# A second series of warm-up products, and the third FFN step in an output bank, in a chunked-attention plus FFN kernel on one core

## Chip, cores and metric

The kernel runs on one core of a Trainium2 chip. The metric is device time in microseconds (us). Before the change the median of three runs is 878.25 us.

## What is computed

Attention inside chunks of 64 positions, then a two-layer FFN on its output (8 batches, 8 heads, 576 positions, head size 64; 4608 tokens, model width 512, FFN width 2048):

```python
scores = (1 / sqrt(64)) * q_c @ k_c.T              # per batch, head and chunk of 64
attn = exp(scores - max); attn = attn / (sum + 1e-9)
x = (attn @ v_c), tokens x 512                     # 4608 x 512
h = x @ w_in                                       # 512 x 2048
g = h if h >= 1; 0 if h <= -1; (h + 1)**2 / 4 between
out = g @ w_out                                    # 2048 x 512
```

## The kernel before

**Tiles.** Tokens go in 9 tiles of 512 (`NTILE`). Each tile has an attention part of 4 head groups (two heads each, `g`) and an FFN part of 16 steps (`j`). An FFN step makes a 128-wide slice of h with 12 TensorE products (`ffn_in`, L532; four groups `kc`, one for each head group, of three products each, since fp32 numbers are split into a high and a low part: xh, xl, and two halves of the weight), the function on it (ScalarE L539 and L542, VectorE L543, then the split into gh, gl at L552 and L553), and two steps later 12 products into four output banks (`ffn_out`, L567, banks ps_o0 to ps_o3).

**Attention of a head group.** Of the first tile: q and k are transposed on TensorE (`flip`, L361, four transposes) and copied to SBUF by ScalarE (L376); 16 small score products (L392, which the trace counts as 32) go into one half of a pair of banks, VectorE takes the maximum (L446) and subtracts it (L462), ScalarE makes the exponential (L465), VectorE the sum and its reciprocal (L471 to L473), GpSimd multiplies (L478). The result e is transposed back (`attn_turn_back`, L361) and copied (L501), 16 value products (L413) go into the other half of the same pair of banks, and ScalarE and VectorE split what comes out into xh (L516) and xl (L517). Two pairs of banks alternate in the first tile: ps_a for even groups, ps_o2 and ps_o3 for odd ones. Of the second tile the exponentials come as eight pieces with their sums (L455). From the third tile on, transposes are done by VectorE.

**Weights.** Each of the 32 weight blocks (wi0 to wi15, wo0 to wo15) arrives as pairs of 32-bit words and is prepared once, on ScalarE (L259, L265, L284) and VectorE (L262, L269, L274, L288; L288 writes the low part and is the last). Until then several tiles of the first attention tile (names `first_...`) lie where late weights will be.

**Order.** `Plan` holds every piece of work with an estimated cost and its needs; its `emit` walks an estimated clock and puts the pieces into the queue of each engine, the earliest first. So each engine's order is fixed at build time, and each engine takes its queue in order. Where TensorE would have nothing to do by the estimate, before the first FFN product, `emit` puts in warm-up products on the identity matrix (L681, into ps_h0, result unused). The order in which the pieces are handed to `Plan` breaks ties: a piece handed in earlier goes first.

In words, before: head group g's value products are handed in right after the scores of group g + 1; the transposes back of the first tile use ps_h1, the bank of the second FFN step; FFN step n uses ps_h0 or ps_h1 by parity; weights are prepared in the order wi0, wi1, wo0, wi2, wo1, wi3, ...

Of the kernel before, what the change touches and what calls it, by code (L numbers as in the profile page):

```python
# [17 lines left out]
class Plan:  # L18
# [9 lines left out]
    def __init__(self):  # L28
        self.parts = []
        self.writer = {}  # L30
        self.readers = {}

    def add(
        self, engine, cost, emit, reads=(), writes=(), lag=0.0, columns=0, port=False, moving=0.0
    ):
        n = len(self.parts)
        needs = {self.writer[k] for k in (*reads, *writes) if k in self.writer}
        for k in writes:
            needs.update(self.readers.pop(k, ()))
            self.writer[k] = n  # L40
        for k in reads:
            self.readers.setdefault(k, []).append(n)
        needs.discard(n)
        self.parts.append((engine, cost, emit, needs, lag, columns, port, moving, writes))

# [15 lines left out]
    def emit(self, filler):  # L61
# [20 lines left out]

        fill_engine, fill_cost, fill_emit, fill_key, fill_columns = filler
        filling = True
        self.columns = {}
        for _ in range(len(parts)):
            while True:
# [12 lines left out]
                start, e = best  # L100
                if filling and free[fill_engine] < start:
                    fill_emit()
                    free[fill_engine] = self.products_end(free[fill_engine], fill_cost, fill_columns)
                    continue
# [3 lines left out]
            n = heapq.heappop(now[e])  # L108
            _, cost, emit, _, lag, columns, port, moving, writes = parts[n]
            filling = filling and fill_key not in writes  # L110
            emit()
            if port:
                start = max(start, port_free)
# [16 lines left out]
def kernel(  # L130
# [15 lines left out]
    nc = tc.nc  # L146
# [18 lines left out]

    FLIPPED = 2

    BATCH = (0, 1, 2, 3, None, 4, 5, 6, 7)
# [131 lines left out]

    def load_rows(dst, src, t, g):

        dst = dst.rearrange("p (c d) -> p c d", d=D)
        for j in range(2):
            nc.sync.dma_start(
                out=dst[j * C:(j + 1) * C],
                in_=heads_rows(src, t, 2 * g + j).rearrange("c p d -> p c d"),
            )

    def load_blocks(dst, src, t, g):  # L310


        dst = dst.rearrange("p (c e d) -> p c e d", e=2, d=Q)
        for j in range(2):
            for i in range(2):
                r = (2 * j + i) * Q
                rows = heads_rows(src, t, 2 * g + j)[:, :, i * Q:(i + 1) * Q]
                if BATCH[t] is not None:
                    nc.sync.dma_start(  # L319
                        out=dst[r:r + Q],  # L320
# [3 lines left out]
                for e in range(2):  # L324
                    nc.sync.dma_start(
                        out=dst[r:r + Q, :, e, :],
                        in_=rows[:, e * Q:(e + 1) * Q, :].rearrange("c p d -> p c d"),
                    )

    def load_values(dst, src, t, g):  # L330

        for h in range(2):
            rows = heads_rows(src, t, 2 * g + h)
            into = dst[:, h * HALF:(h + 1) * HALF].rearrange("p (n d) -> p n d", d=D)
            if BATCH[t] is not None:
                nc.sync.dma_start(out=into, in_=rows.rearrange("(n r) p d -> (r p) n d", r=2))
                continue
            for r in range(2):
                nc.sync.dma_start(
                    out=into[r * C:(r + 1) * C],  # L340
# [3 lines left out]
    def load_heads(t, g, which="qkv"):  # L344
        for n, src, bufs in (("q", q, q_bufs), ("k", k, k_bufs), ("v", v, v_bufs)):
# [5 lines left out]
            if BATCH[t] is None:  # L351
                parts *= 2
            plan.add(
                "sp", 0.67 * parts, lambda load=load, dst=dst, src=src: load(dst, src, t, g),
                (), (key,), lag=2.1, moving=2.2 if load == load_blocks else 1.35,
            )

    def flip(ps, src):
        for u in range(NS):
            cols = slice(u * P, (u + 1) * P)  # L360
            nc.tensor.transpose(out=ps[:, cols], in_=src[:, cols], identity=ident)  # L361

    def attn_turn(t, g):
        for n, (name, bufs, src_bufs, dst_bufs) in enumerate(
# [4 lines left out]
            if t >= FLIPPED:  # L369
# [5 lines left out]
            plan.add("pe", 0.45, lambda src=src, ps=ps: flip(ps, src), (skey,), (pkey,), columns=T)  # L375
            plan.add("act", 0.48, lambda ps=ps, dst=dst: nc.scalar.copy(out=dst, in_=ps),  # L376
                     (pkey,), (dkey,))

# [56 lines left out]
    def attn_softmax(t, g):  # L435
# [39 lines left out]
        plan.add("dve", 0.35 if sums else 1.05, norm, (ekey,), (skey,))  # L475
        on_pool = t < 2
        eng = nc.gpsimd if on_pool else nc.vector
# [4 lines left out]
    def attn_turn_back(t, g):  # L482
# [14 lines left out]

        if t < FLIPPED:
            pkey, ps = h_banks[1] if t == 0 else a_banks[0]
            plan.add("pe", 0.45, lambda: flip(ps, e), (ekey,), (pkey,), columns=T)  # L500
# [21 lines left out]
    def ffn_in(t, j):  # L522
        n = t * NF + j
        pkey, ps = h_banks[n % 2]
        rkey, r = r_bufs[n % 2]
# [82 lines left out]
    for j in range(NF):  # L608
        order.append(("wo", j))
        if j + 2 < NF:  # L610
            order.append(("wi", j + 2))
    for g in range(NP + 1):
        if g < NP:
            attn_turn(0, g)
            attn_products(scores_of(0, g))
            attn_softmax(0, g)
        if g > 0:
            attn_turn_back(0, g - 1)
            attn_products(values_of(0, g - 1))
            attn_split(0, g - 1)  # L620
    loads = [o for o in order if o not in first_loads]
# [12 lines left out]
    prepare("wi", 0)  # L634
    prepare("wi", 1)

    LAG = 2
    todo = list(order)
    for t in range(NTILE + 1):
# [39 lines left out]

    def warm():  # L680
        nc.tensor.matmul(out=h_banks[0][1][:, :P], lhsT=ident, rhs=ident, start=True, stop=True)  # L681

    plan.emit(("pe", 0.215, warm, "ps_h0", 512))


# [29 lines left out]
```

## Time and profile before

| | us |
|---|---|
| timed runs, median (lowest to highest) | 878.25 (877.94 to 878.71) |
| the profiled execution's own time | 878.0 |
| its span in the trace | 876.2 |
| TensorE busy | 860.7 (98%) |
| VectorE busy | 445.0 (51%) |
| ScalarE busy | 382.4 (44%) |

The span is the time from the first to the last instruction of the trace; the device time of the same execution is 1.8 us longer. The span starts with loads, the attention of the first tile and the preparation of the weights; then FFN products follow each other to the end, with the attention of the next tile between them.

### The profile page before, as it was taken

What the parts mean: (1) busy time and instruction counts of PE and PEld (TensorE: products, weight loads), DVE (VectorE), ACT (ScalarE), POOL (GpSimd) and SP (SyncE); (2) the same over time, 40 slices, a digit from 0 to 9 for tenths busy, and PEclk for the clock granted to TensorE, in tenths of its full rate; (3) what the DMA queues carried; (4) which work ended last, traced back from release to release, by engine and by line L of the source; (5) the groups of instructions that cost most, each with busy time, mean ns of one, the idle gap of its engine ahead of it and who ended that gap; (6) DMA issues with size and microseconds to landing.
All of it is one profiled execution on the core that took longest, in us unless ns stands there. A gap on an engine that the chain in (4) does not pass through costs nothing.

```text
span 876.2 us, 14898 instructions
## 1 busy us (share of the span) xinstructions
PE 860.7 (98%) x5942; PEld 707.5 (81%) x5942; DVE 445.0 (51%) x758; ACT 382.4 (44%) x703; POOL 9.9 (1%) x14
## 2 busy tenths in 40 slices
PE   9689999999999999999999999999999999999998
PEld 8577888888888888888888888888888888888886
DVE  4999995444444445444544454444444444423222
ACT  4899964333333333333433333334333433333332
POOL 1001000000000000000000000000000000000000
PEclk9899999999999999999999999999999999999999
DMA  8998215222322224222422243223222311001001
GB/s 195 344 307 238 48 27 116 48 42 42 88 50 39 49 49 97 49 50 49 97 49 48 47 88 53 46 43 89 49 43 46 75 35 25 13 1 49 0 1 49
DMA packets 250821, 62.86 MB, mean 72 GB/s; under 512 B 235904, under 2 KB 244096, under 8 KB 250752
## 3 DMA queue, kind: packets, MB, share of 16 engines
q1 hardware_dynamic: 250752, 61.91, 31.4%
q8 instruction: 47, 0.77, 0.4%
q14 instruction: 22, 0.18, 0.1%
HBM read 45.09 MB, written 9.44 MB: 62 GB/s over the span
## 4 chain that ended last, share of the span: by engine, by line
PE 90%; DVE 3%; DMA 1%; ACT 1%; SPq 1%; issue 1%; POOL 0%; POOLq 0%; DVEq 0%; ACTq 0%
PE ps_o L567 43%; PE ps_h L532 43%; PE ps_a L413 2%; PE ps_a L392 1%; DMA words_wo<-in_moe_w_out_dram 1%; DVE tmp L269 1%; SPq L244 1%; PE ps_a L361 1%; DVE tmp L274 0%; DMA k_sb<-in_k_dram 0%; SPq L319 0%; POOL e L478 0%; ACT tmp L259 0%; DVE mx L446 0%; DVE tmp L262 0%
## 5 line engine op out<-in xcount | busy, mean ns | idle before, releaser
L532 PE MATMUL ps_h<-xh,parts_wi 128*128 128x512 f32 x1152 | 384.9, 394 | 2.1 <-ACT xh L516 1.7
L567 PE MATMUL ps_o<-parts_wo,gh 128*128 128x512 f32 x1152 | 356.1, 390 | 0.0
L532 PEld LDWEIGHTS ps_h<-xh,parts_wi 128*128 128x128 f32 x1152 | 216.8, 188 | 48.8 <-ACT xh L516 1.9
L567 PEld LDWEIGHTS ps_o<-parts_wo,gh 128*128 128x128 f32 x1152 | 216.3, 188 | 44.8
L543 DVE SCALAR_TENSOR_TENSOR r<-ps_h,r 128x512 f32<-128x512 f32 x144 | 98.0, 681 | 266.7 <-ACT r L542 266.7
L532 PE MATMUL ps_h<-xl,parts_wi 128*128 128x512 f32 x576 | 225.1, 391 | 0.8 <-DVE xl L517 0.8
L567 PE MATMUL ps_o<-parts_wo,gl 128*128 128x512 f32 x576 | 224.3, 389 | 0.0
L539 ACT ACTIVATE r<-ps_h 128x512 f32<-128x512 f32 x144 | 86.3, 599 | 285.5 <-PE ps_h L532 285.5
L552 ACT CAST gh<-r 128x512 fp32r<-128x512 f32 x144 | 89.8, 623 | 153.7 <-PE ps_o L567 116.9
L553 DVE TENSOR_TENSOR gl<-r,gh 128x512 fp32r<-128x512 f32 x144 | 98.8, 686 | 109.7 <-ACT gh L552 109.4
L567 PEld LDWEIGHTS ps_o<-parts_wo,gl 128*128 128x128 f32 x576 | 108.3, 188 | 22.7
L532 PEld LDWEIGHTS ps_h<-xl,parts_wi 128*128 128x128 f32 x576 | 108.4, 188 | 22.6 <-DVE xl L517 1.1
L542 ACT ACTIVATE r<-r 128x512 f32<-128x512 f32 x144 | 91.1, 633 | 3.3
L446 DVE TENSOR_REDUCE mx<-ps_a 128x8 f32<-128x512 f32 x34 | 23.4, 690 | 24.2 <-ACT xh L516 13.3
L413 PEld LDWEIGHTS ps_a<-aT,v_sb 64*64 64x64 f32 x1056 | 18.4, 134 | 11.4 <-issue 10.9
L516 ACT CAST xh<-ps_a 128x512 fp32r<-128x512 f32 x34 | 20.0, 588 | 15.3 <-PE ps_a L392 14.6
L471 DVE TENSOR_REDUCE sm<-e 128x8 f32<-128x512 f32 x30 | 20.6, 686 | 10.9 <-ACT e L465 10.9
L413 PE MATMUL ps_a<-aT,v_sb 64*64 64x64 f32 x1056 | 22.9, 224 | 0.0
L517 DVE TENSOR_TENSOR xl<-ps_a,xh 128x512 fp32r<-128x512 f32 x34 | 22.4, 658 | 0.2 <-ACT xh L516 0.2
L392 PE MATMUL ps_a<-kT,qT 64*64 64x64 f32 x1056 | 21.4, 218 | 0.4 <-ACT kT L376 0.4
L504 DVE STREAM_TRANSPOSE x<-e 128x512 f32<-128x512 f32 x28 | 19.9, 711 | 0.9
L370 DVE STREAM_TRANSPOSE qT<-q_sb 128x512 f32<-128x512 f32 x28 | 19.7, 702 | 0.0
(81 smaller groups left out, 391.1 us busy)
## 6 DMA issues: line engine op xcount, KB each, us to landing
words_wi<-in_moe_w_in_dram SPq DMA_DIRECT2D x16, 512.0 KB, 6.8
words_wo<-in_moe_w_out_dram SPq DMA_DIRECT2D x16, 512.0 KB, 7.5
out_dram<-tmp SPq DMA_DIRECT2D x32, 256.0 KB, 2.0
v_sb<-in_v_dram SPq DMA_DIRECT2D x60, 128.0 KB, 2.8
aT<-x SPq DMA_DIRECT2D x224, 32.0 KB, 1.9
q_sb<-in_q_dram SPq DMA_DIRECT2D x96, 64.0 KB, 2.3
k_sb<-in_k_dram SPq DMA_DIRECT2D x96, 64.0 KB, 2.3
q_sb<-in_q_dram SPq DMA_DIRECT2D x12, 128.0 KB, 7.5
```

The source lines that it names most:

```text
L392: nc.tensor.matmul(out=pair[i * C:(i + 1) * C, half, n * C:(n + 1) * C], lhsT=qT[rows, at], rhs=kT[rows, at], start=True, stop=True,)
L413: nc.tensor.matmul(out=pair[h * C:(h + 1) * C, half, HALF + n * C:HALF + (n + 1) * C], lhsT=v_sb[rows, of:of + C], rhs=aT[rows, at:at + C] ...
L446: plan.add("dve", 0.6, lambda: nc.vector.tensor_reduce(out=mx4, in_=sc, axis=AX.X, op=ALU.max), pkeys, (mkey,))
L471: nc.vector.tensor_reduce(out=sm, in_=e3, axis=AX.X, op=ALU.add)
L517: plan.add("dve", 0.6, lambda: nc.vector.tensor_tensor(out=of_tokens(xl), in0=ps, in1=of_tokens(xh.bitcast(F32)), op=ALU.subtract), (*pkey ...
L532: nc.tensor.matmul(out=ps, lhsT=weight["wi", j][:, half, kc * P:(kc + 1) * P], rhs=x, start=(kc == 0 and i == 0), stop=(kc == KC - 1 and i ...
L539: plan.add("act", 0.48, lambda: nc.scalar.activation(out=r, in_=ps, func=AF.Relu, bias=0.5, scale=0.5), (pkey,), (rkey,))
L542: plan.add("act", 0.52, lambda: nc.scalar.square(out=r, in_=r), (), (rkey,))
L543: plan.add("dve", 0.6, lambda: nc.vector.scalar_tensor_tensor(out=r, in0=ps, scalar=1.0, in1=r, op0=ALU.max, op1=ALU.min), (pkey,), (rkey,))
L552: plan.add("act", 0.52, lambda: nc.scalar.copy(out=gh, in_=r), (rkey,), (ghkey,))
L553: plan.add("dve", 0.6, lambda: nc.vector.tensor_tensor(out=gl, in0=r, in1=gh.bitcast(F32), op=ALU.subtract), (rkey, ghkey), (glkey,), port ...
L567: nc.tensor.matmul(out=acc, lhsT=x[:, cols], rhs=weight["wo", j][:, half, :], start=(j == 0 and i == 0), stop=(j == NF - 1 and i == 2),)
```

## The change

1. The loads of k of the first two head groups are issued from ScalarE's queue, ahead of all its other work; SyncE's queue no longer issues them.
2. In the first tile, a head group's transpose back, value products and split are handed in two groups later instead of one (`range(NP + 2)`, `g - 2`), and the transpose back uses ps_o1 and no longer ps_h1.
3. The third FFN step (n = 2, `EARLY`) accumulates in ps_o0; later steps count two banks from there. The first product of wo0 into ps_o0 has to wait until that step has been read.
4. Weights: wi2 is prepared in front of the loop, and in the lists wi(j+2) stands ahead of wo(j).
5. The multiplication of the second tile moves from GpSimd to VectorE (`on_pool`).
6. The warm-up products may come in two series: the first as before until the first FFN product, the second into ps_o0 between the last q copy of the first tile and the opening of the third FFN step.

```diff
-        fill_engine, fill_cost, fill_emit, fill_key, fill_columns = filler
-        filling = True
+        fill_engine, fill_cost, fill_columns, fillers = filler
+        done = {None}
+
+        def fill():
+            for fill_emit, begin, end in fillers:
+                if begin in done and end not in done:
+                    return fill_emit
+            return None
...
-                if filling and free[fill_engine] < start:
-                    fill_emit()
+                if free[fill_engine] < start and fill():
+                    fill()()
...
+    EARLY = 2
...
+            issuer, queue = ("act", nc.scalar) if (n, t) == ("k", 0) and g < 2 else ("sp", nc.sync)
             plan.add(
-                "sp", 0.67 * parts, lambda load=load, dst=dst, src=src: load(dst, src, t, g),
-                (), (key,), lag=2.1, moving=2.2 if load == load_blocks else 1.35,
+                issuer, 0.67 * parts,
+                lambda load=load, dst=dst, src=src, queue=queue: load(dst, src, t, g, queue),
+                (), (key,), lag=2.1, moving=2.2 if load == load_blocks else 1.2,
             )
...
-        on_pool = t < 2
+        on_pool = t < 1
...
-            pkey, ps = h_banks[1] if t == 0 else a_banks[0]
+            pkey, ps = o_banks[1] if t == 0 else a_banks[0]
...
         n = t * NF + j
-        pkey, ps = h_banks[n % 2]
+
+        pkey, ps = o_banks[0] if n == EARLY else h_banks[(n if n < EARLY else n - EARLY - 1) % 2]
...
     for j in range(NF):
-        order.append(("wo", j))
         if j + 2 < NF:
             order.append(("wi", j + 2))
-    for g in range(NP + 1):
+        order.append(("wo", j))
+    for g in range(NP + 2):
         if g < NP:
             attn_turn(0, g)
             attn_products(scores_of(0, g))
             attn_softmax(0, g)
-        if g > 0:
-            attn_turn_back(0, g - 1)
-            attn_products(values_of(0, g - 1))
-            attn_split(0, g - 1)
+        if 1 < g:
+            attn_turn_back(0, g - 2)
+            attn_products(values_of(0, g - 2))
+            attn_split(0, g - 2)
...
     prepare("wi", 1)
+    prepare("wi", 2)
 
     LAG = 2
-    todo = list(order)
+    todo = order[1:]
...
-    plan.emit(("pe", 0.215, warm, "ps_h0", 512))
+    plan.emit(("pe", 0.215, 512, (
+        (warm(h_banks[0][1]), None, plan.written["ps_h0"][0]),
+        (warm(o_banks[0][1]), turned[0], plan.written["ps_o0"][NP]),
+    )))
```

Where it moves instructions. TensorE around the third head group's scores, before: `ps_a` holds even head groups, `first_wi12` and `first_wo13` are the transposed k and q of the later groups, `e0` the exponentials of group 0.

```order
L361 MATMUL ps_o1_114<-ident_63,first_wi14_119 128x128 x4
L681 MATMUL ps_h0_115<-ident_63 128x128 x4
L413 MATMUL ps_a_112<-aT0_78,v_sb0_72 64x64 x16
L681 MATMUL ps_h0_115<-ident_63 128x128 x2
L361 MATMUL ps_o0_113<-ident_63,first_wi15_117 128x128 x4
L681 MATMUL ps_h0_115<-ident_63 128x128 x5
L392 MATMUL ps_a_112<-first_wi12_123,first_wo13_122 64x64 x16
L361 MATMUL ps_h1_116<-ident_63,e1_77 128x128 x4
```

The same place with the change:

```order
L376 MATMUL ps_o1_114<-ident_63,first_wi14_119 128x128 x4
L704 MATMUL ps_h0_115<-ident_63 128x128 x4
L413 MATMUL ps_a_112<-first_wi12_123,first_wo13_122 64x64 x16
L376 MATMUL ps_o1_114<-ident_63,e0_76 128x128 x4
L376 MATMUL ps_o0_113<-ident_63,first_wi15_117 128x128 x4
L704 MATMUL ps_h0_115<-ident_63 128x128 x3
L376 MATMUL ps_o1_114<-ident_63,first_wi14_119 128x128 x4
L704 MATMUL ps_h0_115<-ident_63 128x128 x4
L413 MATMUL ps_o23_111<-first_wi12_123,first_wo13_122 64x64 x16
L376 MATMUL ps_o1_114<-ident_63,e1_77 128x128 x4
L434 MATMUL ps_a_112<-aT0_78,v_sb0_72 64x64 x16
```

The score products of group 2 now stand ahead of group 0's value products on ps_a, those of group 3 ahead of all value products; before, each value product came first.

TensorE from the third FFN step (parts_wi2) on, before; e0 is here the first head group of the second tile:

```order
L532 MATMUL ps_h0_115<-xh2_0_89,parts_wi2_502 128x512
L532 MATMUL ps_h0_115<-xl2_0_97,parts_wi2_502 128x512
L532 MATMUL ps_h0_115<-xh2_0_89,parts_wi2_502 128x512
L361 MATMUL ps_a_112<-ident_63,e0_76 128x128 x4
L532 MATMUL ps_h0_115<-xh3_0_91,parts_wi2_502 128x512
L532 MATMUL ps_h0_115<-xl3_0_99,parts_wi2_502 128x512
L532 MATMUL ps_h0_115<-xh3_0_91,parts_wi2_502 128x512
L567 MATMUL ps_o0_113<-parts_wo0_473,gh0_103 128x512 x2
L567 MATMUL ps_o0_113<-parts_wo0_473,gl0_105 128x512
```

The same with the change, up to that transpose of e0:

```order
L589 MATMUL ps_o1_114<-parts_wo0_534,gl0_105 128x512
L589 MATMUL ps_o23_111<-parts_wo0_534,gh0_103 128x512 x2
L589 MATMUL ps_o23_111<-parts_wo0_534,gl0_105 128x512
L589 MATMUL ps_o23_111<-parts_wo0_534,gh0_103 128x512 x2
L589 MATMUL ps_o23_111<-parts_wo0_534,gl0_105 128x512
L554 MATMUL ps_h0_115<-xh2_0_89,parts_wi3_565 128x512
L554 MATMUL ps_h0_115<-xl2_0_97,parts_wi3_565 128x512
L554 MATMUL ps_h0_115<-xh2_0_89,parts_wi3_565 128x512
L554 MATMUL ps_h0_115<-xh3_0_91,parts_wi3_565 128x512
L554 MATMUL ps_h0_115<-xl3_0_99,parts_wi3_565 128x512
L554 MATMUL ps_h0_115<-xh3_0_91,parts_wi3_565 128x512
L376 MATMUL ps_a_112<-ident_63,e0_76 128x128 x4
```

Ahead of these twelve rows stand the 12 products of wi2 (into ps_o0), the first 6 of wi3 and 2 of wo0. So all of wi3 and 9 products of wo0 now stand ahead of that transpose of e0, where before 3 products of wi2 and all of these stood behind it.

## Rows read from the trace of the kernel before

**Rows 1.** The page: busy time, share of the span, instructions of TensorE.

```profile
PE 860.7 (98%) x5942; PEld 707.5 (81%) x5942; DVE 445.0 (51%) x758; ACT 382.4 (44%) x703; POOL 9.9 (1%) x14
```

**Rows 2.** Windows: stretch, us, busy PE, PEld, DVE, ACT, POOL, granted clock, DMA share, GB/s.

```profile
25.00:30.00 5.00, 2.45 (x41) 1.54 (x39) 4.65 (x10) 4.31 (x8) 0.62 (x1) 0.94 1.20 333
30.00:35.00 5.00, 3.77 (x42) 2.93 (x43) 5.00 (x10) 4.30 (x9) 0.42 (x1) 0.50 1.06 342
35.00:40.00 5.00, 4.62 (x50) 3.64 (x49) 4.60 (x8) 4.03 (x9) 0.00 (x0) 0.87 1.06 404
...
45.00:50.00 5.00, 3.84 (x12) 3.17 (x13) 4.49 (x8) 5.00 (x11) 1.11 (x1) 0.66 0.89 290
50.00:80.00 30.00, 29.30 (x255) 23.56 (x255) 28.03 (x52) 28.78 (x77) 1.29 (x1) 1.00 1.03 318
80.00:110.00 30.00, 29.76 (x197) 23.98 (x196) 29.43 (x55) 29.09 (x69) 2.09 (x2) 1.00 0.35 63
```

**Rows 3.** Timeline, TensorE: start, us, what, count, idle time before and its releaser.

```profile
6.12 0.60 PE L361 MATMUL ps_o<-ident,q_sb 128*128 128x128 f32 x4
...
8.88 0.69 PE L392 MATMUL ps_a<-kT,qT 64*64 64x64 f32 x32
...
10.43 1.06 PE L681 MATMUL ps_h<-ident 128*128 128x128 f32 x8
...
19.05 0.69 PE L392 MATMUL ps_a<-first_wi,first_wo 64*64 64x64 f32 x32
...
24.14 0.69 PE L392 MATMUL ps_o<-first_wi,first_wo 64*64 64x64 f32 x32 [2.05 <-DVE xl L517]
...
33.15 1.13 PE L413 MATMUL ps_o<-first_wi,first_wo 64*64 64x64 f32 x32 [1.23 <-ACT first_wi L501]
...
41.36 0.50 PE L532 MATMUL ps_h<-xh,parts_wi 128*128 128x512 f32 x1 [0.36 <-DVE r L543]
...
46.16 0.84 PE L361 MATMUL ps_a<-ident,e 128*128 128x128 f32 x4 [2.47 <-POOL e L478]
...
72.15 0.66 PE L361 MATMUL ps_a<-ident,k_sb 128*128 128x128 f32 x4 [0.70 <-ACT qT L376]
...
97.46 0.40 PE L532 MATMUL ps_h<-xh,parts_wi 128*128 128x512 f32 x1
```

**Rows 4.** Timeline, VectorE.

```profile
17.88 0.68 DVE L517 TENSOR_TENSOR xl<-ps_a,xh 128x512 fp32r<-128x512 f32 x1
19.81 0.69 DVE L446 TENSOR_REDUCE mx<-ps_a 128x8 f32<-128x512 f32 x1 [1.25 <-PE ps_a L392]
...
22.07 0.69 DVE L471 TENSOR_REDUCE sm<-first_wo 128x8 f32<-128x512 f32 x1 [0.84 <-ACT first_wo L465]
...
44.36 0.20 DVE L473 RECIPROCAL sm<-sm 128x8 f32<-128x8 f32 x1
...
45.13 1.53 DVE L288 TENSOR_TENSOR parts_wo<-tmp,parts_wo 128x512 fp32r<-128x512 f32 x1
...
90.44 0.68 DVE L288 TENSOR_TENSOR parts_wi<-tmp,parts_wi 128x512 fp32r<-128x512 f32 x1
```

**Rows 5.** Timeline, ScalarE.

```profile
25.46 0.59 ACT L501 COPY first_wi<-ps_h 128x512 f32<-128x512 f32 x1 [1.91 <-PE ps_h L361]
...
41.50 0.31 ACT L455 ACTIVATE e<-ps_a,mx 128x64 f32<-128x64 f32 x1
...
43.83 0.66 ACT L552 CAST gh<-r 128x512 fp32r<-128x512 f32 x1
```

**Rows 6.** Timeline, GpSimd.

```profile
23.34 1.05 POOL L478 TENSOR_TENSOR first_wo<-first_wo,sm 128x512 f32<-128x512 f32 x1 [4.48 <-DVE sm L473]
...
44.73 1.38 POOL L478 TENSOR_TENSOR e<-e,sm 128x512 f32<-128x512 f32 x1 [14.31 <-DVE sm L473]
```

**Rows 7.** Chain that ended last: start, us, engine, tile, line, count.

```profile
85.83 2.72 PE ps_h L532 x12
```

**Rows 8.** Timeline, SyncE's queue of loads.

```profile
2.25 1.31 SPq L305 DMA_DIRECT2D k_sb<-in_k_dram  x2
```

More of the change, by code (lines that the diff above doesn't have):

```diff
@@ L31, in __init__ @@
         self.readers = {}
+        self.written = {}
     def add(
@@ L43, in add @@
         needs.discard(n)
-        self.parts.append((engine, cost, emit, needs, lag, columns, port, moving, writes))
+        for k in writes:
+            self.written.setdefault(k, []).append(n)
+        self.parts.append((engine, cost, emit, needs, lag, columns, port, moving))
+        return n
     def products_end(self, start, cost, columns):
@@ L108, in emit @@
             n = heapq.heappop(now[e])
-            _, cost, emit, _, lag, columns, port, moving, writes = parts[n]
-            filling = filling and fill_key not in writes
+            _, cost, emit, _, lag, columns, port, moving = parts[n]
             emit()
+            done.add(n)
             if port:
@@ L299, in heads_rows, with load_rows @@
         return src[:, h, T:, :]
-    def load_rows(dst, src, t, g):
+    def load_rows(dst, src, t, g, queue):
         dst = dst.rearrange("p (c d) -> p c d", d=D)
         for j in range(2):
-            nc.sync.dma_start(
+            queue.dma_start(
                 out=dst[j * C:(j + 1) * C],
@@ L308, in load_rows, with load_blocks @@
             )
-    def load_blocks(dst, src, t, g):
+    def load_blocks(dst, src, t, g, queue):
         dst = dst.rearrange("p (c e d) -> p c e d", e=2, d=Q)
@@ L318, in load_blocks @@
                 if BATCH[t] is not None:
-                    nc.sync.dma_start(
+                    queue.dma_start(
                         out=dst[r:r + Q],
@@ L324, in load_blocks @@
                 for e in range(2):
-                    nc.sync.dma_start(
+                    queue.dma_start(
                         out=dst[r:r + Q, :, e, :],
@@ L328, in load_blocks, with load_values @@
                     )
-    def load_values(dst, src, t, g):
+    def load_values(dst, src, t, g, queue):
         for h in range(2):
@@ L335, in load_values @@
             if BATCH[t] is not None:
-                nc.sync.dma_start(out=into, in_=rows.rearrange("(n r) p d -> (r p) n d", r=2))
+                queue.dma_start(out=into, in_=rows.rearrange("(n r) p d -> (r p) n d", r=2))
                 continue
             for r in range(2):
-                nc.sync.dma_start(
+                queue.dma_start(
                     out=into[r * C:(r + 1) * C],
@@ L375, in attn_turn @@
             plan.add("pe", 0.45, lambda src=src, ps=ps: flip(ps, src), (skey,), (pkey,), columns=T)
-            plan.add("act", 0.48, lambda ps=ps, dst=dst: nc.scalar.copy(out=dst, in_=ps),
-                     (pkey,), (dkey,))
+            copy = plan.add(
+                "act", 0.48, lambda ps=ps, dst=dst: nc.scalar.copy(out=dst, in_=ps),
+                (pkey,), (dkey,),
+            )
+            if t == 0:
+                turned[n] = copy
     def scores_of(t, g):
@@ L678, with warm @@
                 ffn_split(t, j)
-    def warm():
-        nc.tensor.matmul(out=h_banks[0][1][:, :P], lhsT=ident, rhs=ident, start=True, stop=True)
-    plan.emit(("pe", 0.215, warm, "ps_h0", 512))
+    def warm(bank):
+        return lambda: nc.tensor.matmul(
+            out=bank[:, :P], lhsT=ident, rhs=ident, start=True, stop=True
+        )
+    plan.emit(("pe", 0.215, 512, (
+        (warm(h_banks[0][1]), None, plan.written["ps_h0"][0]),
+        (warm(o_banks[0][1]), turned[0], plan.written["ps_o0"][NP]),
+    )))
 _INS = ['q', 'k', 'v', 'moe_w_in', 'moe_w_out']
```

1 line of the change is left out of this document (added).

## Prediction

> **What bounds the kernel now.** I read the page first: TensorE is busy 860.7 of 876.2 us [rows 1]. It works nearly without a gap from the second FFN step to the end, so a change can win only what TensorE loses; the windows show where. From 50 to 110 us it stands still 0.70 and 0.24 us in 30 each [rows 2], but between 25 and 50 us it is idle for long parts, and the granted clock is below 1.00: 0.94, 0.50 and 0.87 in three neighbouring windows, and 0.66 in 45 to 50 us [rows 2]. At two levels, 2.4 and 1.2 GHz, that is 0.6 + 5.0 + 1.3 = 6.9 us at the lower one, and once more 5.0 x 0.34 / 0.5 = 3.4 us. Both follow on idle time: 2.05 us before 24.14 and more up to 33.15, and 2.47 us before 46.16 [rows 3].
>
> The timeline tells what TensorE waits for there. The third group's scores start at 19.05, the fourth's at 24.14 after 2.05 us for an xl, the last values at 33.15 after 1.23 us for a ScalarE copy, and the transpose of the second tile's first e at 46.16 after 2.47 us for GpSimd [rows 3]. These are links of one chain, attention of the first tile and then of the second tile's first group. The prepared weights don't end these waits, but VectorE is busy 4.49 to 5.00 of each 5 us shown and 28.03 and 29.43 of 30 afterwards [rows 2], so it comes next.
>
> **The change, step by step.** I walk the new order with the durations of before. Four transposes take 0.44 us to the next start and 0.60 to their end, four warm-up products 0.99 and 1.06, 16 score or value products 0.62 and 0.69 [rows 3], three FFN products 0.68 (2.72 / 4) [rows 7]; on VectorE a 128x512 operation takes 0.69 and the next starts 0.09 before its end, on ScalarE 0.59 to 0.66 and some 0.1 [rows 4, 5].
>
> *Loads.* Two k loads of 1.31 us each leave SyncE's queue [rows 8], so everything behind them is issued 2.6 us earlier. ScalarE issues them itself; the trace has no load on its queue. At SyncE's price they hold it 2.6 us from its start, before its first copy has anything to copy (the first transposes start at 6.12 [rows 3]); at twice that, 5.2 us, just not. The first warm-up products are as many as before, so transposes still start at 6.12; then only one warm-up product stands between k and q instead of four, and the first scores move from 8.88 to about 8.2. All of the softmax moves by this 0.7.
>
> *Values two groups later.* The third group's scores use ps_a, and before had to follow group 0's values and their xl (VectorE, 17.88 to 18.56 [rows 4]). Now they wait only for their own transposes and copies: 14.8 instead of 19.05. VectorE takes them in turn, maximum at 16.6 instead of 19.81 [rows 4]; the fourth group's scores come at 18.5 instead of 24.14, its subtraction at 20.7, exponential on ScalarE until 22.4, sum and reciprocal 1.1 us (22.07 onwards is such a sum [rows 4]), 23.6; GpSimd 1.05 [rows 6] until 24.9, transposes 25.2, copy 25.9 to 26.5 (such a copy is 0.59 [rows 5]), last values at 26.6 instead of 33.15 [rows 3]. The price is on the first values, now at 19.5, and on the first FFN products, now near 22.8, both later than before; the chain does not wait for either. Eight more warm-up products (39 after 6.12, against 31) lie inside these times.
>
> *Transpose back in ps_o1 and step three in ps_o0.* ps_h1 is free, so the second step's products stand between those of the first. From 27.2 TensorE has work without waits that I can find: wi0 and wi1 are done by 31.7 (before, wi2 starts at 41.36 [rows 3]), wi2 with the second tile's q and k transposes and scores by 36.3, six products of wi3, nine of wo0 (gl, on VectorE by 37.1, is ready in time), six more of wi3: 41.1. The cover of the step in ps_o0 is that order: its release on VectorE, some 44.6, is wanted by wo0's last three products only at 45.
>
> *The multiplication on VectorE.* The second tile's scores end at 35.5; ScalarE has the k copy and seven other pieces first, so its eight exponentials (41.50 to 43.83 before: 2.33 us [rows 5]) run 37.9 to 40.2; then 0.4 for the sums' reciprocal, a weight's L300 0.6 that stands in between, the multiplication 0.69 instead of GpSimd's 1.38 [rows 6]: transposes at 42.2 instead of 46.16. TensorE waits 1.1 us there instead of 2.47. For VectorE the move is about even: it gains 0.60 of work a group and loses a stall, 1.53 us against 0.68 for one L288 beside GpSimd [rows 4].
>
> The Trainium skill (SBUF — State Buffer, Who interferes with whom) says that a VectorE instruction with two SBUF inputs and a GpSimd instruction that reads SBUF shut each other out for a whole instruction. L288 at 45.13 bears that out; if it held to the full, 1.05 or more a group, the move would leave VectorE 0.45 a group better, 1.8 us over four, and rival A below less likely.
>
> *Lead at this place.* TensorE is 46.16 - 42.2 = 4.0 us earlier. It has 57 FFN products behind it (wi0 to wi3 and nine of wo0) instead of 33: 24 x 2.72 / 12 [rows 7] = 5.4 us. And before, 3.4 us at half clock follow, a loss of 1.7. Together 11.1 us.
>
> *What is given back.* VectorE is not 11.1 us ahead. At the reciprocal of this group (40.5 instead of 44.36 [rows 4]) it has five whole weights done instead of six but three more FFN pieces, 0.6 us less in all: it is ahead by 3.9 - 0.6 = 3.2. TensorE's margin to it shrinks by 7.9. The tightest weight that I found is wi10: L288 ends at 91.12, the product that needs it starts at 97.46 [rows 3, 4], 6.3 us. The new order prepares each wi one weight sooner, 0.35 + 3 x 0.60 = 2.1, so 8.4: just enough. But the short pieces of attention, which wait in VectorE's and ScalarE's queues, are tighter. The largest such wait now is 0.70 [rows 3]; one like it for each of four head groups is 2.8, less the 0.9 there now: 1.9 given back. Bounds: 0, if the margins hold, and 7.9, if there were none.
>
> **Sum.** 878.0 - 11.1 + 1.9 = 868.8 against the profiled execution, whose own time this is; the median is 0.25 above it, so **869.0 us**. After 125 us the order is the old one but for the parity of two banks, and the end too.
>
> **Rivals.**
> A. *VectorE takes back more.* From 25 to 110 us it is nearly full, and four multiplications are added to it. For it: 29.43 of 30 us [rows 2]. Against: the margin of 6.3 us at the tightest weight. Halfway from my 1.9 to the bound of 7.9 it takes back 4.9: 872.0.
> B. *The clock falls again.* TensorE still waits 1.1 us before 42.2, and another stretch of 3.4 us at 1.2 GHz costs 1.7: 870.7. For it: 2.47 us of idle brought one [rows 2, 3]. Against: the idle time is less than half as long, and products stand on both sides of it.
> The Trainium skill (TensorE: Matmul & The Clock Gate, What's actually happening) says that the monitor runs free of the kernel's start, so the clock need not change at the same place in each run. By that the lower level could come and go by a stretch, 1.7 us, from run to run. The three timed runs lie within 0.77 us, so nothing here shows it.
> C. *Loads set the pace.* Then the 0.7 us at the first scores is lost, 869.7. The order of loads doesn't change their transfers, only their issue. Against: no wait of TensorE before 21 us is in the trace.
> D. *Slower: the clock stays low.* If from the first FFN product at 22.8 to the second tile's products at 45 TensorE gets 1.2 GHz throughout, 22.2 us of work that I took at full speed last 11.1 longer: 880.1. It decides from 18.4 us at half clock, where half of that is the gain of 9.2. For it: before, 6.9 us of this part are at the lower level [rows 2], and the second series is five products long. Against: the lower level came after idle times of 1.2 to 2.5 us that came close on one another [rows 3], and the walk finds only the one of 1.1.
> E. *No change.* If VectorE or ScalarE give back all of the 11.1, the 7.9 and their own lead of 3.2 as well: 878.
>
> **How the numbers follow.** The forecast (867.2 to 870.4) gets 0.64, A 0.15, B 0.10, C 0.05, D 0.04, E 0.02. The range reaches from nothing given back (878.25 - 11.1 = 867.1) to B on top of a give-back of 4 (878.25 - 11.1 + 4 + 1.7 = 872.9): **867.0 to 873.0**. What a measurement of this kernel can tell from no change is about 0.2%, 1.8 us. Faster 0.94, same 0.02, slower 0.04.
>
> **What would show it.** In the new trace: third group's scores near 14.8, last values near 26.6, the second tile's e transposed near 42; granted clock 1.00 in all windows of 10 to 50 us; waits between 45 and 110 us of 2 to 3 us in sum, on attention pieces and not on weights; four fewer GpSimd multiplications. I am wrong if TensorE is idle for over 5 us between 45 and 110 us (VectorE), if the first copies on ScalarE start after 7 us (loads), or if the windows of 20 to 50 us show 0.50.

## The result and the profile after

| | before | changed |
|---|---|---|
| timed runs, median (lowest to highest), us | 878.18 (877.94 to 878.71) | 869.41 (869.24 to 869.72) |
| the profiled execution's span, us | 876.2 | 867.7 |
| TensorE busy, us | 860.7 | 858.8 |

The ratio is 0.99, 95% interval 0.9883 to 0.9917: 8.8 us faster, where 869.0 was predicted. First the page and the windows of the changed kernel, columns as in [rows 1, 2]:

```profile
PE 858.8 (99%) x5958; PEld 706.9 (81%) x5958; DVE 444.3 (51%) x762; ACT 383.1 (44%) x703; POOL 4.9 (1%) x10
...
25.00:30.00 5.00, 4.77 (x75) 4.00 (x67) 4.92 (x8) 4.52 (x9) 0.60 (x1) 1.00 1.16 306
30.00:35.00 5.00, 4.75 (x26) 3.70 (x25) 5.00 (x11) 4.79 (x10) 0.00 (x0) 1.00 0.98 300
35.00:40.00 5.00, 5.00 (x52) 3.87 (x51) 4.70 (x10) 5.00 (x15) 0.00 (x0) 1.00 1.06 401
40.00:45.00 5.00, 3.97 (x21) 3.06 (x20) 4.72 (x10) 5.00 (x18) 0.00 (x0) 1.00 1.12 300
45.00:50.00 5.00, 5.00 (x24) 4.11 (x23) 4.87 (x10) 5.00 (x11) 0.00 (x0) 1.00 0.85 251
50.00:80.00 30.00, 29.46 (x255) 23.41 (x253) 28.62 (x57) 29.64 (x80) 0.00 (x0) 1.00 1.03 329
80.00:110.00 30.00, 28.77 (x191) 23.19 (x192) 29.29 (x56) 29.68 (x68) 0.00 (x0) 1.00 0.29 53
```

The clock is 1.00 in every window where [rows 2] had 0.94, 0.50, 0.87 and 0.66. From 50 to 110 us TensorE now stands still 0.54 + 1.23 = 1.77 us, where it was 0.94. ScalarE is busy 29.64 and 29.68 of 30 us there, more than VectorE.

The places of [rows 3] in TensorE's timeline, with the idle time before a row and what ended it:

```profile
6.41 0.60 PE L376 MATMUL ps_o<-ident,k_sb 128*128 128x128 f32 x4
...
8.49 0.69 PE L413 MATMUL ps_a<-kT,qT 64*64 64x64 f32 x32
...
15.22 0.69 PE L413 MATMUL ps_a<-first_wi,first_wo 64*64 64x64 f32 x32
...
18.87 0.69 PE L413 MATMUL ps_o<-first_wi,first_wo 64*64 64x64 f32 x32
...
26.03 0.60 PE L376 MATMUL ps_o<-ident,first_wo 128*128 128x128 f32 x4
...
27.75 0.69 PE L434 MATMUL ps_o<-first_wi,first_wo 64*64 64x64 f32 x32 [0.23 <-ACT first_wi L522]
...
43.56 0.63 PE L376 MATMUL ps_a<-ident,e 128*128 128x128 f32 x4 [1.03 <-DVE e L499]
...
64.08 0.63 PE L376 MATMUL ps_a<-ident,e 128*128 128x128 f32 x4 [0.48 <-ACT words_wo L277]
...
80.19 0.63 PE L376 MATMUL ps_a<-ident,e 128*128 128x128 f32 x4 [0.25 <-ACT r L561]
...
95.57 0.66 PE L376 MATMUL ps_a<-ident,k_sb 128*128 128x128 f32 x4 [0.61 <-ACT qT L394]
...
106.94 0.63 PE L376 MATMUL ps_a<-ident,e 128*128 128x128 f32 x4 [0.34 <-DVE e L499]
```

The third and fourth groups' scores come at 15.22 and 18.87 (predicted 14.8 and 18.5), the last values at 27.75 (26.6), the second tile's e at 43.56 (42.2). Each place is later than the walk had it, by 0.4 at first and 1.36 at the end. The row at 26.03 is the last transpose back, which the walk had at 25.2.

How far TensorE is ahead at that e is counted as in the prediction: earlier start, FFN products already done, half clock avoided. The products in front of it are the 48 and 9 of these two rows (windows up to 43.56 us, on the tiles parts_wi and parts_wo alone):

```profile
0.00:43.56 43.56, 12.76 (x48) 1.00 0.99 266
...
0.00:43.56 43.56, 2.21 (x9) 1.00 0.99 266
```

That gives (46.16 - 43.56) + 24 x 2.72 / 12 + 1.7 = 9.7 us of lead; the span gained 876.2 - 867.7 = 8.5, so 1.2 was given back.

### The profile page after: what moved, and what is told of

Its sections match the earlier page's. It is cut to its first block, busy times and chain, and to the rows that moved or that the text cites. A ratio compares the mean times of both kernels' runs of the same rounds, so it can differ in the third digit from the quotient of the medians.

```text
span 867.7 us, 14916 instructions
## 1 busy us (share of the span) xinstructions
PE 858.8 (99%) x5958; PEld 706.9 (81%) x5958; DVE 444.3 (51%) x762; ACT 383.1 (44%) x703; POOL 4.9 (1%) x10
## 4 chain that ended last, share of the span: by engine, by line
PE 90%; ACT 3%; DVE 2%; issue 1%; DMA 0%; SPq 0%; ACTq 0%; DVEq 0%
PE ps_h L554 43%; PE ps_o L589 43%; PE ps_a L434 2%; PE ps_a L413 2%; ACT tmp L271 1%; DVE tmp L281 0%; ACT parts_wi L296 0%; DVE tmp L286 0%; PE ps_a L376 0%; DMA q_sb<-in_q_dram 0%; ACT words_wi L277 0%; ACT e L476 0%; DVE parts_wo L300 0%; ACT gh L574 0%; ACT r L561 0%
## 5 line engine op out<-in xcount | busy, mean ns | idle before, releaser
L499 DVE TENSOR_TENSOR e<-e,sm 128x512 f32<-128x512 f32 x32 | 21.9, 683 | 0.0
```

What stands on the lines that cost most here:

```text
L499: plan.add("pool" if on_pool else "dve", 1.05 if on_pool else 0.6, lambda: eng.tensor_tensor(out=e3, in0=e3, in1=sm.broadcast_to([P, G, C] ...
```

## The experiments

Every edit is to the changed kernel unless it says otherwise. Two medians of these series that are less than some 1 us apart are not told apart: the runs of one kernel spread by 0.5 to 2.2 us.

### One edit undone, and the same edit alone

*e1* hands value products in one group later instead of two, with all else as changed.

```diff
-    for g in range(NP + 2):
+    for g in range(NP + 1):
...
-        if 1 < g:
-            attn_turn_back(0, g - 2)
+        if 0 < g:
+            attn_turn_back(0, g - 1)
...
```

> The changed kernel (869.4 us) with the first tile's values handed in one group later, as before the change; all else as changed. Theory (the attention chain of the first tile): the third group's scores wait again for group 0's xl, near 18 to 19 us instead of 15.2, the last values come at 31 to 33 instead of 27.75, and the time is 4 to 7 us longer, 873.5 to 876.5. Rival (the clock or the earlier loads brought the gain): under 1 us longer, at most 870.4, since both are kept.

Measured: 875.44 us, ratio 0.9964 (0.9951 to 0.9976). 6.0 of the 8.8 us are gone, as the theory had it; the third group's scores start at 18.10 and the last values at 33.61. TensorE's timeline and its windows:

```profile
43.18 0.79 PE L554 MATMUL ps_h<-xh,parts_wi 128*128 128x512 f32 x1 [2.89 <-DVE r L565]
```

```profile
40.00:45.00 5.00, 2.11 (x7) 0.74 1.08 386
45.00:50.00 5.00, 5.00 (x17) 0.57 0.91 145
```

After 2.15 of the 2.89 us of idle time the clock falls (columns here: TensorE busy, clock, DMA share, GB/s), and only 39 products stand ahead of e. The two windows hold 5.0 x 0.26 / 0.5 + 5.0 x 0.43 / 0.5 = 6.9 us at the lower level, so some 3.4 us of this execution's loss are the clock's and not the chain's own.

*e8* is the reverse: the kernel before with this one edit.

```diff
-    for g in range(NP + 1):
+    for g in range(NP + 2):
...
-        if g > 0:
-            attn_turn_back(0, g - 1)
-            attn_products(values_of(0, g - 1))
-            attn_split(0, g - 1)
+        if g > 1:
+            attn_turn_back(0, g - 2)
+            attn_products(values_of(0, g - 2))
+            attn_split(0, g - 2)
```

> The kernel before with one edit: value products handed in two groups later instead of one; loads, banks, weights, warm-up and multiplication as before. Theory (this edit is most of the gain: undone, it cost 6.0 of 8.8 us): last values start at 28 to 30 instead of 33.15, and most of the half clock between 25 and 40 us is gone: 872.5 to 875.5. Rival (it needs the free bank ps_o1 and the third step in ps_o0, without which TensorE finds nothing to do earlier): 876.7 to 878.5.

Measured: 869.91 us, ratio 0.9909 (0.9895 to 0.9922). Both expectations were too slow, though the last values start at 29.22, where the theory had them: this edit alone gives 8.0 of the 8.8 us, and the other five, which alone give 2.8 (e1), add at most 0.5 to it, which is not told apart from nothing. Its timeline of TensorE, and the products ahead of e as above:

```profile
25.41 0.51 PE L532 MATMUL ps_h<-xh,parts_wi 128*128 128x512 f32 x1 [0.28 <-ACT xh L516]
...
26.89 0.50 PE L532 MATMUL ps_h<-xl,parts_wi 128*128 128x512 f32 x1 [0.98 <-DVE xl L517]
...
36.80 0.69 PE L392 MATMUL ps_a<-kT,qT 64*64 64x64 f32 x32 [1.06 <-ACT kT L376]
...
44.32 0.66 PE L361 MATMUL ps_a<-ident,e 128*128 128x128 f32 x4 [0.36 <-POOL e L478]
```

```profile
0.00:44.32 44.32, 11.28 (x39) 1.00 0.93 257
...
0.00:44.32 44.32, 2.88 (x12) 1.00 0.93 257
```

TensorE still waits often, but no single wait after the start is over 1.06 us, the clock is 1.00 in all windows from 10 us on, and 39 + 12 = 51 products stand ahead of e instead of 33: 18 of the 24 that the prediction put down to the banks and the weights' order as well.

### The other edits undone, one at a time

*e2*, k on SyncE's queue:

```diff
-            issuer, queue = ("act", nc.scalar) if (n, t) == ("k", 0) and g < 2 else ("sp", nc.sync)
+            issuer, queue = ("sp", nc.sync)
```

> The changed kernel with all k loads on SyncE's queue again. Theory: only the front moves, as the first scores come later by 0.3 to 0.7 us: 869.6 to 870.3. Rival (loads issued 2.6 us earlier are what pays): 2 us or more longer, 871.4 and up. Third case (two queues share the same transfers, so nothing lands sooner): 869.4 within 0.3.

Measured: 869.37 us, ratio 0.9897 (0.9882 to 0.9912): no difference. The third case had the number, but not the reason: the third group's loads do land later, TensorE waits for one of them, and its scores start at 15.87 instead of 15.22 and the second tile's e at 44.14 instead of 43.56. TensorE's timeline:

```profile
13.09 0.63 PE L376 MATMUL ps_o<-ident,first_wi 128*128 128x128 f32 x4 [0.42 <-DMA first_wi<-in_q_dram]
...
15.87 0.69 PE L413 MATMUL ps_a<-first_wi,first_wo 64*64 64x64 f32 x32
```

So the third group comes later by 0.65 us, at no cost in time that these runs can tell.

*e3*, without the second warm-up series (its line in `fillers` removed):

> The changed kernel without the second series of warm-up products (five of them). Theory: they lie in time in which TensorE would wait anyway: 869.4 within 0.5, granted clock 1.00 from 7 to 50 us. Rival (the clock is held up by them): a stretch at 1.2 GHz between 24 and 50 us and 1.7 us or more longer, 871.1 and up.

Measured: 868.85 us, ratio 0.9892 (0.9877 to 0.9906), just below the theory's range. The clock stays at 1.00 without the series.

*e4*, the second tile's multiplication on GpSimd again (`on_pool = t < 2`):

> The changed kernel with the second tile's four multiplications on GpSimd again. Theory: the first transposes of the second tile's e come about 0.8 us later (GpSimd 1.05 to 1.38 instead of 0.68), VectorE wins and loses about the same: 869.7 to 870.6. Rival (VectorE is the bound from 45 to 110 us and is relieved of 4 x 0.60): 1 to 2.4 us shorter, 867.0 to 868.4.

Measured: 869.78 us, ratio 0.9899 (0.9884 to 0.9914), inside the theory's range, yet 0.4 us is not told apart from nothing. What the theory expected on the way did not come: e is transposed at 42.57, 1.0 us earlier than in the changed kernel and not 0.8 later, in an execution whose first scores started 0.70 earlier (7.79). So the place of e does not price the multiplication.

*e5*, the weights in the old order:

```diff
     for j in range(NF):
+        order.append(("wo", j))
         if j + 2 < NF:
             order.append(("wi", j + 2))
-        order.append(("wo", j))
...
-    prepare("wi", 2)
...
-    todo = order[1:]
+    todo = list(order)
```

> The changed kernel with the weights prepared in the old order (wi0, wi1, wo0, wi2, wo1, wi3, ...). In the changed kernel the low part of wi2 is written at 31.20 and its products start at 32.95; the low part of wi3 is written at 36.47 and its products start at 37.57. One more weight ahead of each puts the writing some 2.4 us later (the distance of the writes at 31.20 and 33.68), so wi2's products can start at 34.5 and wi3's at 39.6: 1.5 to 2.0 us of TensorE time lost. Theory (the earlier wi is part of the gain): of that the wait of 1.03 us before the transposes of e at 43.56 takes up to 1.0, so 870.0 to 871.5. Rival (VectorE's margin is wide, the order does not matter): 869.0 to 869.8. Second rival (the idle time brings a stretch at half clock): 872 or more, with a granted clock below 0.9 in 35 to 50 us.

Measured: 871.64 us, ratio 0.9929 (0.9917 to 0.9942): 2.2 us slower than the changed kernel, a little over the theory's range. Timeline of TensorE, and a window:

```profile
43.31 0.63 PE L376 MATMUL ps_a<-ident,e 128*128 128x128 f32 x4 [2.49 <-DVE e L499]
```

```profile
45.00:50.00 5.00, 5.00 (x18) 3.93 (x17) 4.82 (x9) 4.45 (x9) 0.00 (x0) 0.70 0.99 312
```

The time is not lost at wi2, as the theory said, but where TensorE runs out: 45 products stand ahead of e instead of 57, it waits 2.49 us for e, and half clock follows: 3.4 us at the lower level in the windows of 40 to 50 us (0.96 and 0.70), 1.7 us lost. That is the second rival's mechanism, at less than its price. *e8* has the old order too, and there 51 products stand ahead of e and the clock stays at 1.00. So the old order costs this only beside the other edits; beside which of them is not shown.

*e6*, the transposes back in ps_h1 (`h_banks[1] if t == 0`):

> The changed kernel with the transposes back of the first tile in ps_h1 again, the bank of the second FFN step. The last of these transposes starts at 26.03 and its copy ends near 27.5; the second step's products start after the last values, 27.75, in the changed kernel too. Theory (the bank was not what held the products back once the values come this early): 868.9 to 870.0, last values within 0.7 of 27.75. Rival (the bank matters by itself, as the prediction's walk had it): the second step's products cannot stand between those of the first, TensorE is idle for over 1 us between 22 and 30 us, 870.5 or more.

Measured: 869.89 us, ratio 0.9905 (0.9892 to 0.9919), last values at 28.11: the theory; the bank by itself is worth nothing measurable.

*e7*, the third step in ps_h0, and so no second series:

```diff
-        pkey, ps = o_banks[0] if n == EARLY else h_banks[(n if n < EARLY else n - EARLY - 1) % 2]
+        pkey, ps = h_banks[n % 2]
```

> The changed kernel with the third FFN step back in ps_h0, and so without the second warm-up series, which went into ps_o0 until that step. The step then waits until VectorE has read the first step from ps_h0 (34.88 to 35.56 in the changed kernel), while the first two steps are done by 32.6 and only eight transposes stand in between (0.8 us). Theory (the step in ps_o0 is part of the gain): some 2.0 us of TensorE time lost at 33 to 36, of which the wait of 1.03 us at 43.56 takes 1.0: 870.0 to 871.5. Rival (the transposes of e at 43.56 end the stage whatever stands before them, and what is lost before is made good there or later): 868.5 to 869.7, as the kernel without the second series alone (868.85). Second rival (idle time brings half clock): 872 or more.

Measured: 868.55 us, ratio 0.9894 (0.9879 to 0.9909). The first rival held. Timeline of TensorE:

```profile
42.56 0.63 PE L376 MATMUL ps_a<-ident,e 128*128 128x128 f32 x4 [0.17 <-DVE e L499]
```

57 products stand ahead of e here too. The third step in ps_o0 buys nothing.

### What is given back, and by which engine

In *e9* and *e10* the queues keep their order and a part of one engine's work is left out; *e11* has both edits.

```diff
 e9
+            c = 16 if w == "wi" and j > 3 else T
             nc.vector.scalar_tensor_tensor(
-                out=y, in0=half(1), scalar=0x80000000, in1=y,
+                out=y[:, :c], in0=half(1)[:, :c], scalar=0x80000000, in1=y[:, :c],
 e10
-        plan.add("act", 0.52, lambda: nc.scalar.square(out=r, in_=r), (), (rkey,))
+        c = 16 if t == 0 and j > 2 else T
+        plan.add("act", 0.52, lambda: nc.scalar.square(out=r[:, :c], in_=r[:, :c]), (), (rkey,))
```

> The changed kernel; for the weights wi4 to wi15 VectorE's sign step (L286) works on 16 of the 512 columns, so these weights lose their signs in the other columns. The order of all queues is unchanged. It takes 12 x 0.6 = 7.2 us of VectorE's work out of 40 to 115 us, and nothing of ScalarE's. In the changed kernel 1.2 us of TensorE's lead is given back after 43.56 us. Theory (VectorE gives it back, as the prediction said): idle time of TensorE between 50 and 110 us falls from 1.77 to under 0.8, time 868.0 to 868.6. Rival (ScalarE, busy 29.64 and 29.68 of 30 us, gives it back): 869.1 to 869.7. Third (neither engine's load, only the fixed order): no change here nor in the kernel with the narrow square.

> The changed kernel; in the first tile's FFN steps 3 to 15 ScalarE's square (L564) works on 16 of the 512 columns, so the function is wrong in the others. The order of all queues is unchanged. It takes 13 x 0.53 = 6.9 us of ScalarE's work out of 38 to 115 us, and nothing of VectorE's. Theory (VectorE gives the lead back): 869.1 to 869.7. Rival (ScalarE does: the waits for its copies of qT and its other pieces, 0.48, 0.25 and 0.61 us, go): idle time of TensorE between 50 and 110 us under 0.8, time 868.0 to 868.6. Third (only the order): no change.

> The changed kernel with both: sign step of wi4 to wi15 and square of FFN steps 3 to 15 of the first tile on 16 columns. Both theories with an engine: 867.6 to 868.6. If both engines take part, each alone gives less than 0.6 and both together over 1.0. Third (only the order gives it back): 869.1 to 869.7.

Measured: e9 868.56 us (0.9893, 0.9878 to 0.9908), e10 867.97 (0.9885, 0.9870 to 0.9900), e11 867.01 (0.9877, 0.9861 to 0.9894). Windows of e9, e10 and e11:

```profile
50.00:80.00 30.00, 29.67 (x258) 23.98 (x257) 27.50 (x58) 29.96 (x81) 0.00 (x0) 1.00 1.09 343
80.00:110.00 30.00, 29.22 (x194) 23.59 (x193) 27.10 (x55) 29.66 (x68) 0.00 (x0) 1.00 0.33 59
```

```profile
50.00:80.00 30.00, 29.85 (x260) 24.05 (x260) 29.18 (x59) 28.74 (x82) 0.00 (x0) 1.00 1.09 339
80.00:110.00 30.00, 29.49 (x194) 23.67 (x193) 29.59 (x57) 28.65 (x68) 0.00 (x0) 1.00 0.34 61
```

```profile
50.00:80.00 30.00, 30.00 (x262) 24.52 (x261) 28.48 (x59) 29.46 (x83) 0.00 (x0) 1.00 1.08 337
80.00:110.00 30.00, 30.00 (x198) 24.59 (x196) 28.06 (x59) 28.51 (x69) 0.00 (x0) 1.00 0.35 62
```

TensorE's idle time in these 60 us goes from 1.77 to 1.11, 0.66 and 0.00, the medians from 869.41 down by 0.85, 1.44 and 2.40. The intervals overlap and the runs of e9 and of the changed kernel do as well (867.4 to 869.64 against 869.24 to 869.72); those of e10 and e11 lie below it (up to 868.26 and 867.77).

So ScalarE gives time back: e10 has its rival's idle time and, within 0.03 us, its time. VectorE's share is not shown: e9 has its theory's time but not its idle time, and neither e9's 0.85 us nor e11's 0.96 us against e10 is told apart from nothing; for it speaks only the idle time of one execution each, and between other kernels that differs as much (0.68 us in e8, 1.32 in e2). e11 came out below its range, and e10 alone gave 1.44 us, more than the 0.6 that its rule for two engines allowed. A narrow square also ends its FFN step some 0.4 us sooner (0.23 instead of 0.63 us), which these runs do not separate from ScalarE's load.

*e12* tries to have ScalarE's share without leaving work out: to e7's kernel,

```diff
-        plan.add("act", 0.52, lambda: nc.scalar.square(out=r, in_=r), (), (rkey,))
+        if t == 0 and j > 2 and j % 2:
+            plan.add("pool", 1.05, lambda: nc.gpsimd.tensor_tensor(
+                out=r, in0=r, in1=r, op=ALU.mult
+            ), (), (rkey,), port=True)
+        else:
+            plan.add("act", 0.52, lambda: nc.scalar.square(out=r, in_=r), (), (rkey,))
```

> The kernel without the third step in ps_o0 and without the second series (868.55, the fastest full one so far), with the square of the first tile's FFN steps 3, 5, ... 15 on GpSimd, which does little after 25 us, instead of ScalarE. Nothing is left out. ScalarE loses 7 x 0.53 = 3.7 us of work between 38 and 115 us, about half of what narrow squares took from it (1.44 us faster). Theory (ScalarE's share of what is given back can be had by moving work): 867.5 to 868.2. Rival (GpSimd's squares of over 1 us hold up VectorE's two-input steps, 1.53 us instead of 0.68 in one case of the kernel before, 0.85 us each): VectorE loses up to 6 us, and the time is 868.5 to 870.

Measured: 870.18 us, ratio 0.9908 (0.9892 to 0.9925), 1.6 us slower than e7: the rival, 0.2 us above its range. GpSimd's timeline, then VectorE's:

```profile
46.57 1.06 POOL L565 TENSOR_TENSOR r<-r 128x512 f32<-128x512 f32 x1 [21.43 <-ACT r L561]
...
85.93 5.70 POOL L565 TENSOR_TENSOR r<-r 128x512 f32<-128x512 f32 x1 [11.14 <-ACT r L561]
```

```profile
46.65 1.53 DVE L580 TENSOR_TENSOR gl<-r,gh 128x512 fp32r<-128x512 f32 x1
...
91.67 0.69 DVE L570 SCALAR_TENSOR_TENSOR r<-ps_h,r 128x512 f32<-128x512 f32 x1 [0.94 <-POOL r L565]
```

Beside the first square a VectorE step takes 1.53 us instead of 0.68; the fourth square, beside an unbroken run of nine VectorE steps, seven of them with two SBUF inputs, lasts 5.70 us, and VectorE then waits 0.94 us for it. The Trainium skill (SBUF — State Buffer, Who interferes with whom) has the two shut each other out, and the trace agrees. That this makes up the 1.6 us is not shown: from 50 to 110 us TensorE stands still 2.07 us here and 2.16 in e7, and VectorE's stalls of these rows are 0.85 and 0.94 us. A square takes 1.04 us or more on GpSimd instead of 0.63 on ScalarE, so the FFN steps end later as well.

## Why the prediction was right, point by point

The same count as for the changed kernel, for each kernel whose clock is 1.00 from 40 us on (spans and places of one execution each; "idle" is TensorE's idle time from 50 to 110 us beyond the 0.94 of before):

| kernel | e at | products ahead | lead | span gained | given back | idle |
|---|---|---|---|---|---|---|
| changed | 43.56 | 57 | 2.60 + 5.44 + 1.7 = 9.7 | 8.5 | 1.2 | 0.83 |
| e2, k on SyncE | 44.14 | 57 | 2.02 + 5.44 + 1.7 = 9.2 | 7.9 | 1.3 | 0.38 |
| e8, only the values later | 44.32 | 51 | 1.84 + 4.08 + 1.7 = 7.6 | 7.9 | -0.3 | -0.26 |
| e3, no second series | 42.11 | 57 | 4.05 + 5.44 + 1.7 = 11.2 | 9.6 | 1.6 | 1.24 |
| e4, multiplication on GpSimd | 42.57 | 57 | 3.59 + 5.44 + 1.7 = 10.7 | 9.2 | 1.5 | 1.20 |
| e6, transposes back in ps_h1 | 42.47 | 57 | 3.69 + 5.44 + 1.7 = 10.8 | 9.0 | 1.8 | 0.74 |
| e7, no step in ps_o0 | 42.56 | 57 | 3.60 + 5.44 + 1.7 = 10.7 | 9.3 | 1.4 | 1.22 |
| e12, e7 with squares on GpSimd | 42.71 | 57 | 3.45 + 5.44 + 1.7 = 10.6 | 7.7 | 2.9 | 1.13 |
| e9, narrow sign step | 43.78 | 57 | 2.38 + 5.44 + 1.7 = 9.5 | 9.3 | 0.2 | 0.17 |
| e10, narrow squares | 43.64 | 57 | 2.52 + 5.44 + 1.7 = 9.7 | 9.7 | 0.0 | -0.28 |
| e11, both narrow | 43.56 | 57 | 9.7 | 11.2 | -1.5 | -0.94 |

- **The mechanism held.** The lead at the second tile's e, less what TensorE waits for afterwards, gives the span gained within 0.4 us in seven of the eleven rows. In e11, e2, e6 and e12 0.6, 0.9, 1.1 and 1.8 us stay unexplained. The half clock went, as the sum had it. How the 9.7 us fall to the edits is another matter: there the walk was mostly wrong, as follows.
- **Loads: the front as walked, and worth nothing.** From the first transposes to the first scores pass 2.08 us (6.41 to 8.49), as predicted, and 2.76 before; that they came at 8.49 instead of 8.2 is the first warm-up series, which ended 0.29 later. But SyncE's pairs did not stay at 1.31 us (last section), and e2 prices the whole step at 0.04 us.
- **Values two groups later: right, and nearly the whole.** e1 and e8 agree from both sides. The walk gave this step only the chain's earlier end; it also puts 18 of the 24 further FFN products ahead of e. The first of them starts later (22.04 in e8, 20.52 before), as the walk had it for the changed kernel, but the first steps no longer wait for the last values until 33 us.
- **Banks and third step: the order was read rightly, its worth was not.** In the sum they seemed to carry a part of 5.4 us. e6 and e7 show no loss without them. e7 idles 0.88 + 0.92 = 1.80 us between 25 and 35 us instead of 0.48, and waits 0.17 us for e instead of 1.03: a gap covered earlier only lengthens the wait for e.
- **Weights' order: underrated.** The prediction counted it as margin for wi10 alone. Beside the other edits it is worth 2.2 us (e5), where it keeps TensorE in products until e comes; without them it is not needed for that (e8).
- **Multiplication: right.** "About even" for VectorE: 0.4 us between e4 and the changed kernel, not told apart. That the wait before e is 1.03 us, predicted 1.1, is partly luck: TensorE ran out of products at 42.5 instead of 41.1, as late as e itself.
- **Lead: 9.7 us measured, 11.1 predicted; the term was mis-sized** by e at 43.56 instead of 42.2. Of these 1.36 us, 0.37 are there at the fourth group's scores (18.87 for 18.5, most of it the longer warm-up series), 0.83 at the last transposes back (26.03 for 25.2), 1.15 at the last values. One cause lies in the last stretch. The walk counted no transfers; ScalarE, in whose queue the copy before the last values stands, waited for wi2's words:

```profile
25.48 0.70 ACT L271 ACTIVATE tmp<-words_wi 128x512 f32<-128x512 f32 x1 [1.11 <-DMA words_wi<-in_moe_w_in_dram]
```

e10 has the same queues and not this wait. TensorE's timeline there:

```profile
26.53 0.60 PE L376 MATMUL ps_o<-ident,first_wo 128*128 128x128 f32 x4
...
27.95 0.69 PE L434 MATMUL ps_o<-first_wi,first_wo 64*64 64x64 f32 x32
```

From the transposes to the values it takes 1.42 us where the changed kernel takes 1.72, so the wait costs 0.3 of the 1.36 us. The 0.46 us that are lost between the fourth scores and the last transposes come before that wait; their cause stays open. e3's execution, also without the wait, has last values at 26.50 and e at 42.11, the walk's places, but its first scores came at 7.91, 0.3 earlier than the walk's.

- **Given back: 1.2 us measured, 1.9 predicted.** The two errors, 1.4 and 0.7, are of opposite sign; with the 0.25 for the median they leave 0.4 us, so that the forecast came this close is partly luck. The waits stand where the prediction put them, before attention's transposes (though one ends with a weight's step, words_wo), but sum to 1.77 us instead of 2 to 3. The engine was half named: 1.34 of the 1.68 us in the rows above from 64 us on end with ScalarE, and e10 bears that out.

Of the rivals, A (872.0), D and E are refuted by the time, B by the clock of 1.00. But D's price was too low: 22.2 us of work counted at full speed last 22.2 us longer at half clock, not 11.1, which is the loss in a stretch of 22.2 us at half clock; the refutation does not hang on it. C was right that loads hold pieces up (the 1.11 us, and the 0.42 us in e2) and wrong on the price. A version clearly faster than the changed kernel with all work in it was not found: e7 and e3 have lower medians with fewer edits, but the runs overlap (868.08 to 869.59 and 868.36 to 869.79).

## What to carry to other kernels

Where a program fixes each queue's order, look for the one place where work that nobody waits for stands in front of a chain on a shared buffer: moving it was worth 8.0 of 8.8 us. Price an edit from both sides, alone and undone: five edits that alone gave 2.8 us gave at most 0.5 on top of the one that mattered, and where the others only let TensorE do more before e, it waited there the longer (e7 and the changed kernel). And walk transfers along with the engines, and ask which full engine takes a lead back: here 1.2 us of 9.7 went, and ScalarE was part of it.

## What the runs showed of the hardware that was not expected

**With k issued by ScalarE, SyncE's later pairs are issued more slowly.** ScalarE's and SyncE's queues in the changed kernel, then SyncE's in e2, where it issues all:

```profile
0.73 2.78 ACTq L317 DMA_DIRECT2D k_sb<-in_k_dram  x4
...
4.52 2.02 SPq L317 DMA_DIRECT2D first_wi<-in_q_dram  x2
6.92 1.93 SPq L317 DMA_DIRECT2D first_wi<-in_k_dram  x2
8.89 2.56 SPq L348 DMA_DIRECT2D v_sb<-in_v_dram  x2
11.50 2.11 SPq L317 DMA_DIRECT2D first_wi<-in_q_dram  x2
```

```profile
6.98 1.28 SPq L317 DMA_DIRECT2D first_wi<-in_q_dram  x2
8.30 1.31 SPq L317 DMA_DIRECT2D first_wi<-in_k_dram  x2
9.66 2.54 SPq L348 DMA_DIRECT2D v_sb<-in_v_dram  x2
12.24 1.28 SPq L317 DMA_DIRECT2D first_wi<-in_q_dram  x2
```

The same pairs take 2.02 and 1.93 us instead of 1.28 and 1.31, later 2.11 instead of 1.28, so of 2.46 us by which SyncE is ahead at 4.52 only 0.74 are left at 11.50. The slow pairs are issued after ScalarE's loads, which end at 3.51, and the kernel before, with all loads on SyncE, has such a pair too (1.91 us at 11.26); so it is not two queues issuing at the same time. That transfers still under way hold up the issue would fit (DMA share 1.34 from 4.5 to 6.9 us, 0.84 from 4.5 to 7 in e2), but is not shown. The Trainium skill (DMA: Bandwidth & Descriptors, Issuing engines are not separate DMA queues) says that the transfers run on the same engines whoever issues them and only issue time is saved; here most of the issue time that was saved was lost again.

**The first warm-up series is not always equally long.** The same 24 products from 1.36 us on take 4.93 us in the kernel before, 5.21 in the changed one, 5.49 in e10 and 4.37 in e11, and the first transposes follow between 5.57 and 6.63 us. The Trainium skill (TensorE: Matmul & The Clock Gate, What's actually happening) has the monitor run free of the kernel's start; the granted clock reads 1.00 from the first product on in all four, so no row here shows that the difference is the clock's. The end does not follow it: e11, 0.84 us ahead of the changed kernel at the first transposes, has its e at 43.56 as well.

**Which waits came before half clock.** In the kernel before, the granted clock fell first near 29.4 us, some 5 us after the wait of 2.05 us [rows 3], after one more of 1.73 and during one of 0.82, and again near 46.5, just after the one of 2.47. In e1 it fell near 42.4, 2.15 us into the wait of 2.89, and in e5 near 44.6, 1.2 us after the one of 2.49. After e8's waits of up to 1.06 us, six within 20 us, it stayed at 1.00. The first of these falls, then e1's, in windows of 1 us (columns: TensorE busy, clock, DMA share, GB/s):

```profile
29.00:30.00 1.00, 0.17 (x2) 0.72 1.50 263
```

```profile
42.00:43.00 1.00, 0.00 (x0) 0.72 1.08 395
```
